# A grouped 1x1 convolution on one core: every full slot is stored in two halves

## The chip, the cores and the metric

The kernel runs on one core of one Trainium2 chip. The metric is the device time of one execution, in microseconds (us). Three executions of the kernel before took 477.21, 481.44 and 481.57 us, so its median is 481.44 us. One more execution was taken with the hardware profiler; it took 478.2 us, and all durations below are from that one.

## The reference

Inputs are an image `x` of 1 x 512 x 512 pixels with 192 channels in bf16, and weights `w` of 4 groups, 48 x 48 each. The kernel size is 1, so each pixel is by itself: its 192 channels are 4 groups of 48, and each group is multiplied by its own 48 x 48 matrix.

```python
B, H, W, C = x.shape                     # 1, 512, 512, 192
xg = xp.reshape(B, H, W, G, Cg)          # G = 4, Cg = 48, no padding
out = jnp.einsum('bhwgc,gcd->bhwgd', xg, w[0, 0])
return out.reshape(B, H, W, C)
```

There are 262,144 pixels of 384 bytes: 100.7 MB are read and 100.7 MB are written.

## The kernel before

**The ring.** All data passes through one buffer in SBUF, `ring`, of 128 partitions and 520 columns. A column is one pixel (384 bytes) in each partition. The ring is cut into 5 slots of 104 columns. The image is cut into pieces (`plan_pieces`), and the pieces fill the slots in turn: slot number n of the run lies in place n modulo 5. Slot 0 comes in four pieces of 8, 24, 32 and 40 columns (`HEAD`). Slots 6 and 13 are made of a piece of 40 columns and a "shared" piece, whose 64 columns lie in only some of the partitions. The last slot, number 20, has 36 columns. The 17 others are full: one piece of 104 columns each, 128 rows of 39,936 bytes, 4992 KB.

**What happens to a piece.** It is loaded into its place in the ring. TensorE (PE) takes it in groups of 4 columns: it transposes the group's channels into PSUM (L287), VectorE copies them to SBUF as `xT_sb` (L337), TensorE multiplies them by the weights into `o_ps` (L301), and ScalarE (ACT) copies the result back over the same four columns of the ring (L364). When enough columns have been written over, they are stored to the output. There are 529 groups. TensorE works on pairs of groups, and transposes one pair ahead of the pair that it multiplies.

**Who issues the transfers.** SP issues all loads but the shared ones, in order (L249). ACT issues all stores but the shared ones, in its own instruction stream, a group or two after the last copy that they need (L358). POOL issues the loads and stores of the two shared pieces (L221, with some tiny transfers at L219 ahead of them). The three have a DMA queue each: q1 for SP, q10 for ACT, q0 for POOL. Any transfer over 128 partitions is spread over the core's 16 DMA engines, 8 partitions each, and every engine serves all three queues.

**What waits for what.** A load may only write columns of the ring whose old contents have been stored: before it issues the load of piece p, SP waits (`wait_free`) for every store that covers the columns which p takes over from five slots before. `store_of` says which store covers which group. POOL does the same for a shared piece, two pieces ahead of the one in hand. POOL also collects the landings: it waits for a piece's load and then raises `ready` (L234), on which TensorE waits before its first transpose of the piece. POOL runs through the pieces in order, so a wait for a shared piece's place stands ahead of the report on the piece in hand.

**How stores are cut.** The list `stores` is made once, ahead of everything (lines 142 to 154). A piece is stored whole, with two exceptions: the last piece goes in parts of 16, 12 and 8 columns, and a full piece of the last three slots (`LATE = 3`) goes in two halves. Of the full slots that is true of numbers 18 and 19. The list decides what ACT issues and after which group, and how many semaphores SP and POOL wait for.

The functions that the change touches, with the line numbers of the profile:

Of the kernel before, what the change touches and what calls it, by code (L numbers as in the profile page):

```python
# [25 lines left out]
SLOT = 104  # L26
# [1 line left out]
COLS = SLOTS * SLOT  # L28
COL = 2 * C
HEAD = (8, 24, 32, 40)  # L30
LATE = 3
LAST_PARTS = (16, 12, 8)
LOOP = 2 * SLOT // 4
SHARED_AT = (6, 13)
# [48 lines left out]
def plan_pieces(npix):  # L83
    few = sum(rows * cols for _, rows, _, cols, _ in SHARED)
    at = list(SHARED_AT)
    if npix < len(at) * few + 128 * SLOT * (1 + at[-1]):
        at = []
    cols = (npix - few * len(at)) // 128
    assert cols % 4 == 0
    pieces, g, pix, n = [], 0, 0, 0  # L90
    while cols:
        if n in at:
            parts = [(SLOT - WIDE, None), (WIDE, SHARED)]
        elif n == 0 and cols >= SLOT:
            parts = [(s, None) for s in HEAD]
        else:
            parts = [(min(SLOT, cols), None)]
        for s, shares in parts:
            pieces.append(Piece(len(pieces), n, g, s, shares, pix))
            cols -= 0 if shares else s  # L100
            g, pix = pieces[-1].g1, pieces[-1].pix_end
        n += 1
    assert pix == npix
    return pieces


def bass_standalone__grouped__vision_kernel(nc, x, w, out):
# [5 lines left out]
    pieces = plan_pieces(npix)  # L113
# [27 lines left out]

    stores = []
    for p in pieces:
        late = pieces[-1].slot - p.slot
        half = p.size // 8 * 4
        parts = (p.size,)
        if p is pieces[-1] and p.size == sum(LAST_PARTS):
            parts = LAST_PARTS
        elif p.full and late < LATE and half:
            parts = (p.size - half, half)  # L150
        c = 0
        for n in parts:
            stores.append((p, c, c + n, p.g0 + (c + n) // 4))
            c += n
# [245 lines left out]
```

## Time and profile before

| | |
|---|---|
| median of three executions | 481.44 us (477.21 to 481.57) |
| profiled execution | 478.2 us |
| its span, first to last instruction | 476.2 us |
| TensorE clock granted, mean | 0.981 of full speed |
| busy: PE / ACT / VectorE | 435.7 / 398.7 / 254.1 us |
| moved by DMA | 201.50 MB, 423 GB/s over the span |
| full stores, 4992 KB | 15, median 46.7 us from issue to landing |
| half stores, 2496 KB | 4, median 22.5 us from issue to landing |
| full loads, 4992 KB | 17, median 33.8 us from issue to landing |

How to read the profile: it is of one execution on the core. PE is the matmul, PEld the weight load that goes beside it, DVE is VectorE, ACT ScalarE, POOL GpSimd; a name with q (SPq, ACTq) is the engine's instruction queue, where waits and DMA issues stand. "Busy tenths" cut the span into 40 equal slices, and each digit is the busy share of a slice in tenths, 9 being 90% or more. A line of waits reads: engine, what it was about to write, its line, an arrow to what ended the wait, and then the total us, the number of waits and the longest. A line of DMA issues reads: out<-in, the queue, how many, KB of each, and the median us from the issue to the landing of the last byte. KB are 1024 bytes, MB and GB are powers of ten.

### The profile page before, as it was taken

To read this page: it belongs to the slowest core of one execution; us is meant where nothing else is said; L and a number is where in the kernel's file an instruction comes from. 1 tells how busy PE (TensorE), PEld (TensorE's weight loads), DVE (VectorE), ACT (ScalarE), POOL (GpSimd) and SP (SyncE) were. 2 spreads that over 40 slices of the span, in tenths; PEclk is the share of its full clock that TensorE was granted. 3 is DMA by queue.
4 is the path that set the end of the run, shared out by engine and by line. 5 is a ranking of instruction groups with operands and counts; after the bars stand their busy time and mean duration, and the time that the engine had idled before them with its cause. 6 is when DMAs were issued, how large, how long until landed. Compare 5 with 4: busy or idle time off the path is not lost.

```text
span 476.2 us, 14571 instructions
## 1 busy us (share of the span) xinstructions
PE 435.7 (92%) x6358; PEld 394.8 (83%) x6358; DVE 254.1 (53%) x266; ACT 398.7 (84%) x530; POOL 10.0 (2%) x23
## 2 busy tenths in 40 slices
PE   5998899999999999999999999999998998988970
PEld 5887798888989888898888889889888897878860
DVE  2645455655555565555555555555554654554630
ACT  2988799989998998999899899989996998786980
POOL 1000000010000010000001000010000000000000
PEclk9999999999999999999999999999998999998995
DMA  8999999999999999999999999999999999999996
GB/s 345 430 432 426 427 436 438 429 418 424 423 413 429 430 443 426 425 438 433 433 429 430 434 437 424 436 429 437 423 404 437 429 423 426 423 438 439 413 431 284
DMA packets 8571, 201.50 MB, mean 423 GB/s; under 512 B 1664, under 2 KB 1664, under 8 KB 2304
## 3 DMA queue, kind: packets, MB, share of 16 engines
q1 hardware_dynamic: 3456, 97.72, 48.1%
q10 hardware_dynamic: 4240, 97.73, 47.9%
q0 software_dynamic: 864, 5.91, 3.0%
q8 instruction: 6, 0.10, 0.1%
q14 instruction: 5, 0.04, 0.0%
HBM read 100.69 MB, written 100.66 MB: 423 GB/s over the span
## 4 chain that ended last, share of the span: by engine, by line
PE 65%; DMA 22%; another core or an unknown queue 7%; issue 2%; ACT 1%; SPq 0%; POOL 0%; POOLq 0%
PE o_ps L301 38%; PE xT_ps L287 27%; DMA ring<-in_x_dram 13%; DMA out_dram<-ring 8%; ACT ring L364 1%; SPq L249 0%; POOL cur L219 0%; POOL out_dram L221 0%; POOLq L234 0%; SPq L55 0%
## 5 line engine op out<-in xcount | busy, mean ns | idle before, releaser
L364 ACT CAST ring<-o_ps 128x768 bf16<-128x768 f32 x529 | 397.4, 802 | 62.9 <-PE o_ps L301 55.4
L337 DVE COPY xT_sb<-xT_ps 128x1536 bf16<-128x1536 bf16 x265 | 253.4, 956 | 201.3 <-PE xT_ps L287 201.3
L301 PE MATMUL o_ps<-wt,xT_sb 128*128 128x144 bf16 (+1 forms) x3174 | 294.8, 235 | 7.5 <-issue 2.6
L301 PEld LDWEIGHTS o_ps<-wt,xT_sb 128*128 128x128 bf16 x3174 | 213.7, 98 | 45.4 <-ACT ring L364 30.2
L287 PE MATMUL xT_ps<-ident,ring 128*128 128x128 bf16 x3174 | 223.6, 221 | 14.5 <-POOLq L234 10.1
L287 PEld LDWEIGHTS xT_ps<-ident,ring 128*128 (+1 forms) x3174 | 192.2, 99 | 17.4 <-issue 17.2
L219 POOL DMA_DIRECT2D cur<-in_x_dram x7 | 4.2, 597 | 309.0 <-DMA out_dram<-ring 182.4
L261 PE MATMUL o_ps<-w_sb,esel 48*128 48x48 bf16 x10 | 0.6, 210 | 4.3 <-DMA w_sb<-in_w_dram 4.3
L261 PEld LDWEIGHTS o_ps<-w_sb,esel 48*128 48x128 bf16 x10 | 0.5, 110 | 4.2 <-issue 4.2
L331 DVE CAST wt<-o_ps 128x480 bf16<-128x480 f32 x1 | 0.7, 658 | 4.9 <-PE o_ps L261 4.9
L364 ACT ACT_TABLE_LOAD x1 | 1.3, 1283 | 1.3 <-PEq L385 1.3
L221 POOL DMA_DIRECT2D ring<-in_x_dram x4 | 2.3, 582 | 0.0
L221 POOL DMA_DIRECT2D out_dram<-ring x4 | 2.3, 576 | 0.0
L205 POOL TENSOR_SCALAR_AFFINE_SELECT esel<-esel 48x272 bf16<-48x272 bf16 x1 | 0.4, 402 | 0.0
L202 POOL MEMSET esel<- 48x272 bf16 x1 | 0.3, 317 | 0.3 <-POOLq L385 0.3
L209 POOL TENSOR_SCALAR_AFFINE_SELECT ident<-ident 128x128 bf16<-128x128 bf16 x1 | 0.3, 282 | 0.0
L203 POOL MEMSET ident<- 128x128 bf16 x1 | 0.2, 198 | 0.0
L385 POOL MEMSET const-float32-0.0<- 128x1 f32 x1 | 0.1, 98 | 0.3 <-issue 0.3
L385 POOL MEMSET const-bfloat16-1.0<- 128x1 bf16 x1 | 0.1, 101 | 0.0
L385 POOL MEMSET const-uint8-127<- 128x1 uint8 x1 | 0.1, 101 | 0.0
L385 POOL MEMSET const-float32-1.0<- 128x1 f32 x1 | 0.1, 98 | 0.0
## 6 DMA issues: line engine op xcount, KB each, us to landing
ring<-in_x_dram SPq DMA_DIRECT2D x17, 4992.0 KB, 33.8
out_dram<-ring ACTq DMA_DIRECT2D x15, 4992.0 KB, 46.7
out_dram<-ring ACTq DMA_DIRECT2D x4, 2496.0 KB, 22.5
ring<-in_x_dram SPq DMA_DIRECT2D x3, 1920.0 KB, 30.0
out_dram<-ring ACTq DMA_DIRECT2D x3, 1920.0 KB, 55.8
ring<-in_x_dram POOLq DMA_DIRECT2D x2, 1056.0 KB, 23.0
out_dram<-ring POOLq DMA_DIRECT2D x2, 1056.0 KB, 30.4
ring<-in_x_dram SPq DMA_DIRECT2D x1, 1728.0 KB, 29.8
```

Source lines behind the costliest of these rows:

```text
L202: gp.memset(esel[:], 1.0).then_inc(p0_sem, 1)
L205: gp.affine_select(out=esel[:], in_=esel[:], pattern=[[-1, ECOLS]], compare_op=AluOpType.is_equal, fill=0.0, base=ESHIFT, channel_multipli ...
L209: gp.affine_select(out=ident[:], in_=ident[:], pattern=[[-1, 128]], compare_op=AluOpType.is_equal, fill=0.0, base=0, channel_multiplier=1) ...
L219: gp.dma_start(cur[0:n, turns[0]], few).then_inc(cur_sem, 16)
L221: gp.dma_start(*((sbuf, dram) if inward else (dram, sbuf))).then_inc(done, 16)
L261: last = pe.matmul(o_ps[:, NOB - 1, col:col + CG], lhsT=esel[:, s0:s0 + 128], rhs=w_sb[:, g, :], start=True, stop=True, skip_group_check=True)
L287: last = pe.transpose(xT_ps[:, g % NXP, i * 128:(i + 1) * 128], xs, ident[:])
L301: last = pe.matmul(o_ps[:, v % NOB, c0_:c1_], lhsT=xs[:, i * 128:(i + 1) * 128], rhs=wt[:, WOFF[tc]:WOFF[tc] + (c1_ - c0_)], start=(tc == ...
L331: dve.tensor_copy(wt[:], o_ps[:, NOB - 1, 0:WCOLS]).then_inc(wc_sem, 1)
L337: dve.tensor_copy(xT_sb[pair % NXS][:, 0:n * 2 * UC].rearrange("p (g c) -> p g c", g=n), xT_ps[:, b0:b0 + n, 0:2 * UC]).then_inc(e_left, 1)
L364: act.copy(dst, o_ps[:, v % NOB:v % NOB + 2, 0:UC]).then_inc(o_left, 1)
L385: nc = _bacc.Bacc("TRN2", target_bir_lowering=False, num_devices=1)
```

## The change

The two halves are no longer kept for the last slots. Every piece that fills a slot of 104 columns is stored as two parts of 52 columns; the constant `LATE` goes. The last piece keeps its parts of 16, 12 and 8, and the pieces of the first slot, the 40 columns of slots 6 and 13 and the shared pieces are stored as before.

```diff
-LATE = 3
 LAST_PARTS = (16, 12, 8)
...
     stores = []
     for p in pieces:
-        late = pieces[-1].slot - p.slot
         half = p.size // 8 * 4
         parts = (p.size,)
         if p is pieces[-1] and p.size == sum(LAST_PARTS):
             parts = LAST_PARTS
-        elif p.full and late < LATE and half:
+        elif p.full and p.size == SLOT:
             parts = (p.size - half, half)
         c = 0
         for n in parts:
             stores.append((p, c, c + n, p.g0 + (c + n) // 4))
             c += n
```

ACT's stream has 15 more DMA issues: each of 15 full slots (numbers 1 to 5, 7 to 12 and 14 to 17) has one after its 13th group and one after its 26th, where it had one after the 26th. A half is 128 rows of 19,968 bytes. The streams of the other engines hold the same instructions. The lines behind the change move up by two. A load of a full slot now waits for two stores of the slot five before it; the 40 columns of slots 6 and 13 and the 36 of slot 20 wait for the first half of it alone.

## The prediction

> **What bounds the kernel now.** I read the slices first, then the DMA queues, then the waits, then stretches of my choosing. The slices and the queues, from the page:
>
> ```profile
> PE   5998899999999999999999999999998998988970
> DMA  8999999999999999999999999999999999999996
> ...
> q1 hardware_dynamic: 3456, 97.72, 48.1%
> q10 hardware_dynamic: 4240, 97.73, 47.9%
> q0 software_dynamic: 864, 5.91, 3.0%
> ```
>
> q1 carries SP's loads, q10 ACT's stores, q0 POOL's shared pieces. The shares add to 99.1% of the span (with 0.1% for instructions): the 16 DMA engines work 471.9 of 476.2 us. Of the 4.3 us left, some 2.6 lie before the first load moves. PE is busy too (92%), and the chain that ended last is 65% PE, which tempts one to call PE the bound. But PE ends at 462.0 us and the last store lands some 13 us later, and PE waits for loads near the end. The waits from 340 us on:
>
> ```profile
> PE xT_ps L287 <- POOLq L234: 8.2, 3, 3.1
> ```
>
> L234 is POOL's report that a piece has landed, and the chain shows the last of these to be the load issued at 391.90 that landed at 429.5. So PE waits for DMA, not DMA for PE. Stretches (columns: stretch, its length, busy time by engine, granted TensorE clock, DMA share, GB/s):
>
> ```profile
> 3.00:12.30 9.30, 6.88 (x74) 6.54 (x75) 3.41 (x4) 2.02 (x3) 0.00 (x0) 1.00 1.04 428
> 165.00:208.00 43.00, 41.97 (x624) 38.10 (x622) 24.68 (x27) 38.83 (x52) 2.28 (x4) 1.00 1.01 434
> 300.00:350.00 50.00, 48.85 (x728) 44.33 (x726) 28.86 (x31) 45.23 (x61) 2.27 (x4) 1.00 0.99 422
> 400.00:445.50 45.50, 39.36 (x560) 35.64 (x557) 22.34 (x24) 35.05 (x47) 0.00 (x0) 0.96 1.00 428
> 445.50:465.00 19.50, 15.80 (x224) 13.70 (x222) 8.87 (x10) 15.81 (x22) 0.00 (x0) 1.00 1.01 430
> ```
>
> The first row is loads alone (the first store is issued at 12.29), the last is stores alone (the last load lands at 445.5), the others are mixed: 428, 430 and 422 to 434 GB/s. So the engines move about 429 GB/s whatever the mix, and the time is bytes over that rate plus two short ends. The change moves the same bytes.
>
> **How two queues share an engine.** While the long loads of slots 1 to 4 run, the four small stores of slot 0 go beside them. Single issues, sizes and times to landing:
>
> ```profile
> out_dram<-ring ACTq DMA_DIRECT2D x1, 384.0 KB, 16.9
> out_dram<-ring ACTq DMA_DIRECT2D x1, 1152.0 KB, 26.9
> out_dram<-ring ACTq DMA_DIRECT2D x1, 1536.0 KB, 35.8
> out_dram<-ring ACTq DMA_DIRECT2D x1, 1920.0 KB, 42.9
> ```
>
> Issued at 12.29, 17.33, 23.86 and 33.12, they land at 29.2, 44.2, 59.7 and 76.0. The four loads (issued at 2.6 to 4.3, 26.4, 40.9, 55.8 and 71.7 us to landing) land at about 29, 44, 59 and 76: each store ends with one load, though it has a tenth to two fifths of its bytes. At half the bandwidth 0.39 MB would have taken 1.8 us, not 16.9. So each engine takes turns, a row of a store, a row of a load. A DMA has 144 packets (3456 over 24 loads), 9 an engine: 8 rows and one for the semaphore.
>
> **The change part by part.**
>
> *Turns.* The 15 full slots that were stored whole get rows of 19,968 B instead of 39,936. An engine moves 429/16 = 26.8 GB/s: 1.49 us a full row, 0.74 a half. Before, a load got every second row of equal size; its 8 rows need 8 x 2.98 = 23.8 us, and with the load ahead of it in the queue the median load lands after 33.8 us. After, a turn of both is 2.23 us: 8 turns are 17.9, with start and semaphore some 20 to 22 us. In that time only one half slot is stored; the other half, 8 x 0.74 = 5.9 us, then goes alone. 17.9 + 5.9 = 23.8, the old period. No byte is saved: loads land earlier, and since the bytes are the same, stores land later, by about half a slot's store, 6 us.
>
> *Who waits for the later stores.* SP's load of a slot waits for both halves of the slot five before, so it is issued about 6 us later and lands (33.8 - 21) - 6, some 7 us, earlier than now. The first pieces of slots 6 and 13 and the last load need the first half alone, which helps a little. POOL, before it reports slot 12 as landed, must wait for the whole store of slot 8 (it lands at 255.4 now, 261 then); PE needs slot 12 at about 274, so 12 us of cover stay. Slot 5's report waits likewise for slot 1 (96.4 now; its second half then some 10 us later), and is needed at about 122. Were that cover gone, PE would wait, with some two slots of stores (46.7 us to landing) still queued for the DMA engines.
>
> *PE.* With loads 7 us earlier the three late waits (8.2 us) go, and the slow matmuls after them (granted clock 0.66 from 430 to 435). PE ends some 7 us earlier. What is late next is the DMA queue: those 7 us become a longer drain, so I take nothing for it. At most what is idle behind the first load, 4.3 - 2.6 = 1.7 us, could be had.
>
> *ACT.* 15 more issues of 338 ns are 5.1 us on ACT, which idles 62.9. In the steady part ACT needs 2 x 0.773 us for a pair that takes PE 1.635 (two pairs every 3.27 us in the chain), so one issue is made up in four pairs; a half slot has 6.5. PE and DVE have the same instructions. Were that cover gone, PE would lose 5.1 us, less than the 13 us by which the last landing follows it.
>
> *15 more DMAs on q10*, 135 packets more on each engine. The nearest row is the half stores that run already, one behind the other at the end:
>
> ```profile
> out_dram<-ring ACTq DMA_DIRECT2D x1, 2496.0 KB, 25.0
> out_dram<-ring ACTq DMA_DIRECT2D x1, 2496.0 KB, 20.0
> ```
>
> Issued at 434.73 and 445.61, they land at 459.7 and 465.6 (the next at 471.5): 5.9 us apart for 2.556 MB, 433 GB/s. So a half store queued behind another costs nothing that shows. Upper bound in a queue: the second load, 24 columns, lands 3.14 us after the first; 1.18 MB at 429 are 2.75, so 0.39 a DMA, or 5.9 us for 15. Far bound: the first load, with nothing ahead of it, took 3.1 us for 0.92 us of bytes: 2.2 of its own, 33 us for 15. Below nothing: 433 against 429 is 0.9% on a quarter of the time, -1.0 us. I take +0.03 each, +0.5 us, by the nearest row, and keep -1 and +5.9 for the range.
>
> The Trainium skill (DMA: Bandwidth & Descriptors, "Anatomy of one DMA") gives every DMA a fixed cost of about 2.0 us; the lone first load agrees with its 2.2. Paid 15 times in line, that would be 30 us and a time of some 510. The page lays most of it to waiting for the last byte's receipt, and the queued half stores at 5.9 us agree that the next DMA hides it.
>
> **Sum.** Against the profiled execution of 478.2 us (span 476.2): bytes 0, PE 0, ACT 0, DMAs +0.5: 478.7. The runs shown are 477.21, 481.44 and 481.57, their mean 480.1, 1.9 above the profile. I lay the sum on that: 480.6, rounded to 480.5, 0.2% under the median. The three runs lie 0.9% apart, so 1% (4.8 us: under 476.6 or over 486.3) is about what can be told from no change.
>
> **Rivals.**
>
> *A, faster: the rate rises.* The late stretch with its PE waits runs at 422 (300 to 350) and 428 (350 to 445), the middle at 433 to 434. If loads in time lift these to 433, that is 50 x 11/433 + 95 x 5/433 = 2.4 us; with the 1.7 idle and the forecast's 0.5 not paid, 480.1 - 4.1 = 476.0. For it: a run with steadier loads might also fall nearer to the fastest of the three. Against: DMA share is 1.00 in the dips too. Chance 0.17.
>
> *B, slower: an added store costs its own time.* In the stretches where stores now run alone (5.9 us of every 23.8) no load fills a gap between one half and the next. It decides from (486.3 - 480.1)/15 = 0.41 us an added store, just above the 0.39 of the queued load and far below the 2.2 of the lone one. At 0.5 us: 487.6. For it: those stretches are new in the middle of the run. Against: the half stores 5.9 us apart, in just such a stretch. All of the skill's 30 us I give 0.01 of this case's 0.18.
>
> *C, the turns don't follow the rows*: engines share by bytes when both queues are long, loads still take some 33 us, and PE's three waits stay. DMA is as full as before: 480.5 again. Chance 0.10; the four pairs of landings speak against it.
>
> The forecast itself has 0.55. Faster: A, 0.17. Slower: B, 0.18. Within 1%: forecast and C, 0.65. The likeliest case alone spans 477 to 485 (the spread of the runs, and -1 to +3). For 8 in 10 I go out to A and B as priced: 474.5 to 488.
>
> **What the changed profile would show.** 34 stores of 2496 KB where there are 4, and none of 4992 KB. Median load to landing 20 to 24 us instead of 33.8. Late PE waits for L234 near zero, PE's last matmul at 453 to 457. DMA share still 9 in every slice, 423 GB/s over the span within 1%. q10 with 15 x 144 = 2160 packets more, 6400, and its share within half a point of 47.9%. Wrong would be a slice of DMA below 9 in the middle, q10's share up by over 1 point (B), or a mean over 428 GB/s (A).

## The result, and the profile after

| | before | after |
|---|---|---|
| median of twelve executions | 476.59 us (475.40 to 481.57) | 482.47 us (480.73 to 483.55) |
| ratio to before | | 1.0101, 95% interval 1.0070 to 1.0133 |
| profiled execution | 478.2 us, span 476.2 | 482.83 us, span 480.9 |

The change makes the kernel 1.0% slower. The number forecast, 480.5 us, lies near the measured one and the range holds it, but the forecast was for no change that can be told, and it rested on three executions of before that turned out to be high ones. Between the two profiled executions the forecast was +0.5 us and the measured difference is +4.6 us; the medians of twelve lie 5.9 us apart. (The ratios here leave out executions of a kernel that fell over 1.5% behind its fastest; the profiles of experiments 5 and 15 are of such executions, and only their packets are read.)

The page of after, the span in 40 slices and the DMA queues (packets, MB, share of 16 engines):

```profile
span 480.9 us, 14605 instructions
...
PE   4989799999999999999999999999999599999920
...
DMA  8999999999999999999999999999999999999994
...
DMA packets 10731, 201.50 MB, mean 419 GB/s; under 512 B 1904, under 2 KB 1904, under 8 KB 2544
...
q1 hardware_dynamic: 3456, 97.72, 47.9%
q10 hardware_dynamic: 6400, 97.74, 47.8%
q0 software_dynamic: 864, 5.91, 2.9%
```

As before, DMA stands at 9 in every slice to the last; q10 has the 2160 more packets that were forecast, and its share has not grown. And yet the mean rate is 419 GB/s instead of 423. By this page the engines are as busy as they were and move less. The one slice that differs is the last: 4 instead of 6.

The same page's DMA issues (how many, KB each, median us from issue to landing):

```profile
ring<-in_x_dram SPq DMA_DIRECT2D x17, 4992.0 KB, 23.8
out_dram<-ring ACTq DMA_DIRECT2D x34, 2496.0 KB, 50.3
```

The loads land after 23.8 us instead of 33.8, which is the turn by rows as the prediction has it. But a half store now takes 50.3 us, longer than a whole one took (46.7). PE's waits from 340 us on, and from the timeline the longest of them with the issue of the load it waited for:

```profile
PE xT_ps L285 <- POOLq L232: 5.1, 2, 4.8
```

```profile
360.67 7.75 SPq L247 DMA_DIRECT2D ring<-in_x_dram  x2
...
384.69 1.36 PE L285 MATMUL xT_ps<-ident,ring 128*128 128x128 bf16 x12 [4.75 <-POOLq L232]
```

One long wait, of 4.8 us, is left: PE stands still until the load of slot 17, issued at 360.67, has landed at 384.3. Before, that load was issued at 351.79.

The stretches of after that answer to those shown of before, and then its last 9 us (columns: stretch, length, busy time by engine, granted TensorE clock, DMA share, GB/s):

```profile
165.00:208.00 43.00, 41.93 (x624) 38.00 (x622) 24.67 (x27) 38.90 (x52) 2.29 (x4) 1.00 1.00 427
300.00:350.00 50.00, 48.85 (x728) 44.34 (x726) 28.73 (x30) 45.25 (x62) 2.28 (x4) 1.00 1.01 429
400.00:445.50 45.50, 44.39 (x659) 40.16 (x657) 26.51 (x28) 41.16 (x56) 0.00 (x0) 1.00 1.00 426
445.50:465.00 19.50, 13.84 (x197) 11.99 (x195) 7.56 (x9) 14.06 (x19) 0.00 (x0) 0.96 1.02 435
472.00:474.00 2.00, 0.00 (x0) 0.00 (x0) 0.00 (x0) 0.00 (x0) 0.00 (x0) 0.50 0.78 320
474.00:476.00 2.00, 0.00 (x0) 0.00 (x0) 0.00 (x0) 0.00 (x0) 0.00 (x0) 0.50 0.34 139
476.00:478.00 2.00, 0.00 (x0) 0.00 (x0) 0.00 (x0) 0.00 (x0) 0.00 (x0) 0.50 0.16 67
478.00:480.90 2.90, 0.00 (x0) 0.00 (x0) 0.00 (x0) 0.00 (x0) 0.00 (x0) 0.50 0.04 18
```

and the last 6 us of before:

```profile
470.00:472.00 2.00, 0.00 (x0) 0.00 (x0) 0.00 (x0) 0.00 (x0) 0.00 (x0) 0.50 0.76 313
472.00:474.00 2.00, 0.00 (x0) 0.00 (x0) 0.00 (x0) 0.00 (x0) 0.00 (x0) 0.50 0.38 155
474.00:476.00 2.00, 0.00 (x0) 0.00 (x0) 0.00 (x0) 0.00 (x0) 0.00 (x0) 0.50 0.11 44
```

Between 165 and 208 us, where PE is as busy as before, the rate fell from 434 to 427 GB/s. The last rows are the first sign of where the time went. A share of 1/16 is 0.06: from 476 us on, one to three of the 16 engines work, and the others have ended. In after this tail runs from 474 to 480.4 us, in before from 472 to 475.7. So a mean over 16 engines was the wrong thing to look at.

### Engine by engine

The trace lists each packet with its queue, size, start and duration, but not its engine. The packets can be laid out on 16 engines, so that each engine does one after the other (with some 3 ns of overlap from one to the next, which makes a busy time up to 2 us longer than the time it fills) and takes its own 8 rows of every transfer, in order. In this layout, made from 4.6 us on, no engine is ever idle for more than 1.3 us before its last store. What is said of single engines below rests on it; the landings are read directly from the semaphores' updates, of which each transfer has one per engine.

An undisturbed row of 39,936 bytes takes 1476 ns, a half row of 19,968 takes 742, the semaphore's packet 9 (the commonest durations). With these every engine has a fixed amount of work. What its packets take beyond that is called its *stall* here.

```
profiled executions, us, from 4.6 us on           before                  after
mean of 16 engines: fixed work                     464.5                   465.7
                    stall                            4.4                     5.8
                    instruction fetches              0.5                     0.4
                    busy, the sum                  469.4                   471.9
busiest engine:     fixed work                     465.4                   466.5
                    stall                            5.5                    10.1
                    instruction fetches              1.4                     0.9
                    busy, the sum                  472.4                   477.5
time of the execution less the busiest engine        5.8                     5.3
last store lands, first / median / last engine     471.1 / 472.7 / 475.7   472.4 / 474.7 / 480.4
slot 12's store,  first / median / last engine     342.2 / 346.9 / 351.8   337.6 / 350.0 / 360.6
```

The fixed work grows by 1.1 us: 120 more half-row pairs by 8 ns and 15 more semaphore packets by 9 ns on each engine. The rest of the +4.6 us is stall, and it counts where it is largest: the busiest engine lost 5.5 us before and 10.1 after, while the median of the 15 ordinary ones went from 2.7 to 4.7. (A sixteenth engine, of which more at the end, stalls 19 us in both and is spared the shared pieces.) The profiled execution of before lies 1.6 us above its median, so a usual one has probably stalled less: the same stores with another first slot (experiment 12 below, 475.53 us) lose 2.9 us on the worst ordinary engine. The row of slot 12 shows the same lag in the middle of the run, and what it does to PE: SP may issue the load of slot 17 only when the *last* engine has stored slot 12, at 360.6 us, though half the engines had stored it by 350.0.

The stalls are not spread evenly. Rows of two engines are often slow together: after 70 us, 114 rows of after (the sixteenth engine's left out) are stalled by 200 ns or more, 44.9 us together. Of this, 61% is on rows that have a partner, a row of the same queue on another engine at the same time and slowed about as much; with the times of the other engines shifted by 5 to 55 us, 1 to 20% would have one. In before it is 77 rows, 32.2 us, 73% with a partner. At the worst both take twice their time: at 125.8 us two half rows take 742 + 779 ns each. So such pairs hold most of the long stalls of both kernels. But of the 12.7 us that after adds in such rows they are only 3.9 (61% of 44.9 less 73% of 32.2); for the rest no partner was found.

### The profile page after: what moved, and what is told of

The parts are those of the page before. It is cut to its first block, busy times and chain, and to the rows that moved or that the text cites. A ratio compares the mean times of both kernels' runs of the same rounds, so it can differ in the third digit from the quotient of the medians.

```text
span 480.9 us, 14605 instructions
## 1 busy us (share of the span) xinstructions
PE 434.6 (90%) x6358; PEld 393.8 (82%) x6358; DVE 254.0 (53%) x266; ACT 398.7 (83%) x530; POOL 10.0 (2%) x23
## 3 DMA queue, kind: packets, MB, share of 16 engines
q10 hardware_dynamic: 6400, 97.74, 47.8%
## 4 chain that ended last, share of the span: by engine, by line
PE 53%; another core or an unknown queue 23%; DMA 17%; issue 2%; ACT 1%; SPq 0%; POOLq 0%
PE o_ps L299 31%; PE xT_ps L285 22%; DMA out_dram<-ring 10%; DMA ring<-in_x_dram 6%; ACT ring L362 1%; SPq L247 0%; SPq L54 0%; POOLq L232 0%
## 5 line engine op out<-in xcount | busy, mean ns | idle before, releaser
L299 PEld LDWEIGHTS o_ps<-wt,xT_sb 128*128 128x128 bf16 x3174 | 212.7, 98 | 46.7 <-ACT ring L362 30.9
## 6 DMA issues: line engine op xcount, KB each, us to landing
ring<-in_x_dram SPq DMA_DIRECT2D x17, 4992.0 KB, 23.8
out_dram<-ring ACTq DMA_DIRECT2D x34, 2496.0 KB, 50.3
ring<-in_x_dram SPq DMA_DIRECT2D x3, 1920.0 KB, 23.8
```

The lines of the kernel that those rows point to most:

```text
L299: last = pe.matmul(o_ps[:, v % NOB, c0_:c1_], lhsT=xs[:, i * 128:(i + 1) * 128], rhs=wt[:, WOFF[tc]:WOFF[tc] + (c1_ - c0_)], start=(tc == ...
```

## The experiments

Each ran with the kernel before on the same chip; ratios are to that. The letters in the expectations are the theories as they stood when they were written, and each text says what it expects. The diffs show the lines that matter; "..." stands for lines left out.

### 1, 2: equal rows for loads, and a later issue for stores

Loads of full slots in halves too, both after the same waits:

```diff
+    def load_parts(p):
+        return ((0, SLOT // 2), (SLOT // 2, SLOT)) if p.full and p.size == SLOT else ((0, None),)
...
                 wait_free(wq, p)
-                for _, dram, sbuf in transfers(xf, p, SYNC):
-                    sp.dma_start(sbuf, dram).then_inc(ld_sem[p.i], 16)
+                for c0, c1 in load_parts(p):
+                    for _, dram, sbuf in transfers(xf, p, SYNC, c0, c1):
+                        sp.dma_start(sbuf, dram).then_inc(ld_sem[p.i], 16)
```

> The full loads are cut into two halves as well, so that a row of a load and a row of a store are equal again (19,968 B). Theory T (turns): the loss of the changed kernel comes from stores getting the smaller row in each turn; the store queue grows, the 16 engines drift apart in it (the last store's slowest engine lands 5.7 us after the median engine, 3.0 before). With equal rows loads take some 34 us again, the slowest engine ends about 3 us behind the median, and only the fixed cost of rows stays, 2 x 1.1 us: ratio to the kernel before 1.003 to 1.006. Theory R (rows): each added row and semaphore packet costs, in its fixed 8 to 9 ns and in longer stalls, 4 to 5 us for 2160 packets; with twice as many the ratio is 1.015 to 1.025.

Halves as in after, but both issued at the end of their slot:

```diff
         for n in parts:
-            stores.append((p, c, c + n, p.g0 + (c + n) // 4))
+            due = p.g1 if len(parts) == 2 and p.slot < 18 else p.g0 + (c + n) // 4
+            stores.append((p, c, c + n, p.g0 + (c + n) // 4, due))
...
-                while todo and todo[0][3] < g:
+                while todo and todo[0][4] < g:
```

> Halves as in the changed kernel, but for slots 1 to 17 both are issued together after the slot's last group, as the whole store was. Theory T and theory R: the rows are the same, so the ratio stays 1.007 to 1.013 and loads land in some 24 us. Rival E (early issue): what costs is that the first half is issued ten us sooner and sits beside the load; then the ratio falls to 1.000 to 1.004.

Experiment 1 measured 1.0100 (1.0053 to 1.0147), between the ranges of T and R; one of its five executions took 485.50 us, and the four others, at 478.64 to 479.90, are 0.5 to 0.8% above the median of before. Experiment 2 measured 1.0154 (1.0136 to 1.0171), above every range written down for it. From the page of experiment 1, the slices of DMA and the issues:

```profile
DMA  8999999999999999999999999999999999999977
...
ring<-in_x_dram SPq DMA_DIRECT2D x34, 2496.0 KB, 53.8
out_dram<-ring ACTq DMA_DIRECT2D x34, 2496.0 KB, 22.4
```

With equal rows the roles turn: the half loads wait in their queue (53.8 us) and the stores go through quickly. The stalls are gone, a median of 1.3 us an engine instead of 4.7, and the engines land the last store within 475.0 to 476.9 us. But PE now waits 16.9 us for loads:

```profile
PE xT_ps L289 <- POOLq L235: 16.9, 6, 5.6
```

so PE's last matmul ends at 469.4 us instead of 462.0, and the engines run out of stores before it (columns as above; the share of the DMA engines is 0.31):

```profile
460.00:465.00 5.00, 4.83 (x72) 4.18 (x70) 2.84 (x4) 4.41 (x7) 0.00 (x0) 1.00 0.31 132
```

So the gain is given back. Experiment 2 keeps the 23.8 us of the loads and the stalls (7.6 us on the worst engine). It isn't the early issue of the first half that costs: issued late, the halves cost more, 1.0154 against 1.0101.

### 3, 9, 13, 14: halves in a part of the run

```diff
-        elif p.full and p.size == SLOT:
+        elif p.full and p.size == SLOT and (p.slot < 10 or p.slot >= 18):       # 3: slots 1 to 9
+        elif p.full and p.size == SLOT and p.slot >= 10:                        # 9: slots 10 to 19
+        elif p.full and p.size == SLOT and (p.slot < 5 or p.slot >= 18):        # 13: slots 1 to 4
+        elif p.full and p.size == SLOT and (5 <= p.slot < 10 or p.slot >= 18):  # 14: slots 5 to 9
```

(Slots 18 and 19 are in halves before, too.)

> Halves for slots 1 to 5 and 7 to 9 only (and 18 and 19, as before); slots 10 to 17 are stored whole. Theory T: from slot 10 on turns are equal again, the engines' distance at the end is that of the kernel before (3 us from median to last), ratio 1.000 to 1.004. Theory R: half of the added rows, half of the loss, 1.004 to 1.007.

> The complement of the early halves: slots 1 to 9 are stored whole, slots 10 to 19 in halves. With early halves alone the loss was whole (1.0137) and the last engine's lag was there before slot 10. If lags come only from the loads that begin on an empty queue, each costs alike and the late half brings its share: worst engine's stalls 7 to 10 us, ratio 1.004 to 1.010. If the early part of the run is what matters (first fills, the shared piece at 97 us), the late half costs little: 1.000 to 1.004.

> Only slots 1 to 4 in halves, beside 18 and 19. T (a load that begins on an empty queue costs the engines about 0.3 us on the mean and the unluckiest about 1 us, so the loss goes with the number of such loads): the loads of slots 5 to 9 alone begin on an empty queue, 4 of the 7 to 8 that the kernel with slots 1 to 9 in halves has before 300 us; ratio 1.004 to 1.009, the loads that follow directly stalled under 0.1 us. U (once the engines have been put out of step early in the run, the rest follows by itself): ratio 1.010 to 1.015, as with slots 1 to 9, and stalls go on after the last load that began on an empty queue.

> Only slots 5 to 9 in halves, beside 18 and 19. T: loads of slots 10 to 14 begin on an empty queue, the other half of those; ratio 1.004 to 1.009, and the two parts together come near the 1.0137 of slots 1 to 9. U: what counts is that it begins early; ratio 0.998 to 1.004, as with the late halves (1.0019).

```
halves in slots        added stores   ratio (95% interval)        us lost per added store
1 to 9    (3)                     8   1.0137 (1.0119 to 1.0155)   0.82
10 to 19  (9)                     7   1.0019 (0.9996 to 1.0042)   0.13
1 to 4    (13)                    4   1.0113 (1.0090 to 1.0136)   1.35
5 to 9    (14)                    4   1.0067 (1.0041 to 1.0093)   0.80
all       (after)                15   1.0101 (1.0070 to 1.0133)   0.32
```

(Loss: the ratio's excess by the 476 us of before.) Experiment 3 went against everything expected of it: the early half of the change alone carries the whole loss. Issues in the page of experiment 9, then of experiment 3:

```profile
ring<-in_x_dram SPq DMA_DIRECT2D x17, 4992.0 KB, 29.6
```

```profile
ring<-in_x_dram SPq DMA_DIRECT2D x17, 4992.0 KB, 29.2
```

The loads land as early in both, and yet 3 loses 6.5 us and 9 loses 0.9 (for 9, the second of the two cases in its text). The packets agree: the worst ordinary engine stalls 9.2 us in experiment 3, nearly all of it before 300 us, and 3.8 in experiment 9. Four slots at the start cost as much as all fifteen. Against their expectations: 1 to 4 came out as U had it (set off early), not as T had it (in proportion to the loads begun on an empty queue); 5 to 9 came out as T had it, not as U; and the two together exceed the 1.0137 of both. So the loss neither goes with the number of half stores nor is set off only at the very start. It is the dearer, the earlier the halves come. The profiled execution of experiment 13 was the fastest of its six (478.41, median 481.40), so its packets, 5.9 us on the worst engine, show little of that loss.

### 4: the mirror, loads in halves and stores whole

The edit of experiment 1, on the kernel before.

> The other way round: full loads in halves, stores as in the kernel before. Theory T: stores get the larger row, full loads take 40 us and more, TensorE waits for loads on every slot from the middle of the run on, and the store queue runs short; slower than the changed kernel, ratio 1.01 to 1.03. Theory R: 17 x 144 added packets, about the same as the changed kernel's 2160, ratio 1.008 to 1.013, whatever the queue they are on.

It measured 1.0321 (1.0299 to 1.0343), a little above T's range and far above R's. Waits, and the slices of the page:

```profile
PE xT_ps L291 <- POOLq L237: 27.6, 5, 9.5
```

```profile
DMA  8999999999999999999999999999999999999557
...
ring<-in_x_dram SPq DMA_DIRECT2D x34, 2496.0 KB, 48.0
out_dram<-ring ACTq DMA_DIRECT2D x15, 4992.0 KB, 23.2
```

Now the stores have the long rows and two thirds of each engine, as the turns by row say: 23.2 us, and the loads 48.0. Loads are what PE needs, so PE waits 27.6 us, and the queue of stores runs dry. The stalls come too: a median of 8.3 us on an engine, 13.3 on the worst. Unequal rows come with stalls whichever way round they are.

### 6, 7: equal rows without PE's waits

Experiment 6 is 1, with each half load waiting for the half store alone that it replaces:

```diff
-                wait_free(wq, p)
...
                 for c0, c1 in load_parts(p):
+                    wait_free(wq, p, c0, c1)
...
```

> Loads and stores of full slots in halves, and each half load waits only for the half store whose place it takes, so that loads are issued half a slot sooner than where both halves of a load wait for both stores. Theory S: q1 never runs dry, load rows lose 0.01 to 0.05 us an engine; what kept the kernel with both in halves at 1.01 were 16.9 us of TensorE waits for late loads and idle DMA engines at the end (2 to 4 us each). These shrink to under 10 and under 2 us: time 474 to 478, ratio 0.997 to 1.004. Theory R (rows): 1.008 to 1.02, as with both in halves.

Experiment 7 makes every full slot of two pieces, so that loads, waits, reports to PE and stores all go by 52 columns (and the shared pieces are issued three pieces ahead, not two):

```diff
-AHEAD = 2
+AHEAD = 3
...
-            parts = [(min(SLOT, cols), None)]
+            parts = [(SLOT // 2, None)] * 2 if cols >= SLOT else [(cols, None)]
```

> Full slots are made of two pieces of 52 columns each: loads, stores, the waits for free places and TensorE's waits for landed data all go by halves (POOL looks three pieces ahead instead of two, to issue the shared loads where it did). Theory S as above, and TensorE starts on a half as soon as it has landed, 12 us sooner than on the whole: TensorE waits under 5 us in the second half of the run, DMA engines idle under 1 us before the end, time 473.5 to 477, ratio 0.994 to 1.001. Theory R (rows): 1.008 to 1.02.

Experiment 6 measured 1.0052 (1.0009 to 1.0094), with 14.6 us of PE's waits for loads left where S expected under 10 (one of its six executions took 483.06 us, the others 477.96 to 479.42). Experiment 7 measured 1.0000 (0.9966 to 1.0033), as S had it. GB/s in the 40 slices, experiment 7, then before, then after:

```profile
GB/s 347 416 412 434 427 428 433 435 432 427 430 432 432 427 430 429 430 433 432 428 432 427 431 431 426 430 430 432 426 426 431 436 432 433 432 428 427 430 430 286
```

```profile
GB/s 345 430 432 426 427 436 438 429 418 424 423 413 429 430 443 426 425 438 433 433 429 430 434 437 424 436 429 437 423 404 437 429 423 426 423 438 439 413 431 284
```

```profile
GB/s 340 457 411 430 422 432 415 414 419 431 424 424 422 421 433 423 434 440 420 428 447 401 433 425 427 427 430 425 424 425 441 443 417 427 420 421 432 438 422 194
```

From the fifth slice to the one before the last, experiment 7 stays within 426 to 436; before dips to 404 and after to 401, and from the seventh slice to the fourteenth, 72 to 168 us, after lies at 414 to 431. Such stretches are part of the loss, and "9" in the slices of DMA hides them. All stores and loads of experiment 7 are halves, so its rows cost 2.3 us more of fixed work than before's, and it makes them good: the median stall is 1.2 us. So half rows by themselves, and more of them and more DMAs than in after, do not cost what after loses. Unequal rows do, or what comes with them: in after the load queue, and in experiment 4 the store queue, also runs empty at times, and these runs do not part the one from the other.

### 10, 11, 12: is it chance of timing?

After and before with the first slot's pieces in another order (10 and 12), and after with parts of 56 and 48 columns (11):

```diff
-HEAD = (8, 24, 32, 40)
+HEAD = (8, 24, 40, 32)
```

```diff
-        half = p.size // 8 * 4
+        half = 48
```

> The changed kernel with the last two pieces of slot 0 swapped (8, 24, 40, 32 columns): the same bytes, rows and DMAs, a little other timing. Theory P: what costs is that rows of two engines meet and slow each other to as little as half speed, the engine that meets most often sets the end, and which engines meet hangs on where they stand to one another when loads begin anew. Then a shift without work changes the loss by 2 us and more in at least one of this run and the next two: ratio anywhere in 1.000 to 1.020, and the profiled time is the worst engine's busy time plus 5 to 6 us. Theory S (each load on an empty queue costs a set time): 1.007 to 1.013.

> The changed kernel with parts of 56 and 48 columns instead of 52 and 52: the same number of rows and DMAs. Theory P: 1.000 to 1.020, not the same loss but by chance; stalls of 200 ns and more still come mostly two engines at a time. Theory S: 1.007 to 1.013.

> The kernel before with the same swap in slot 0. Its loads follow one another without a gap for most of the run. Theory P: fewer meetings, but some around the shared pieces and late loads: 0.995 to 1.008, likely moved by 1 us or more. Theory S: 0.998 to 1.002.

They measured 1.0114 (1.0086 to 1.0142), 1.0103 (1.0076 to 1.0131) and 0.9968 (0.9935 to 1.0002). P wanted the loss to move by 2 us or more in one of them, and it did not (against after's 1.0101 the first two lie within 0.6 us, and the third is 1.5 us under before); S's range holds for 10 and 11. Which engines meet when is different in each, but the loss of the halves stays where it was, and the kernel with whole stores stays at before's time (0.3% under it, which isn't resolved; no kernel here is shown to be faster than before). The worst ordinary engine stalls 10.1, 10.5 and 2.9 us. So it isn't an unlucky timing of this one program.

All kernels whose packets were laid out, by their profiled executions:

```
                        time     busiest engine   time - busiest   stall of the 15: median, max
before                  478.20   472.4            5.8              2.7    6.9
after                   482.83   477.5            5.3              4.7   10.1
1  both in halves       479.30   472.3            7.0              1.3    4.7
2  late issue           482.07   476.3            5.8              5.3    7.6
3  slots 1 to 9         482.47   476.7            5.8              4.7    9.2
4  loads in halves      494.03   480.9           13.1              8.3   13.3
6  half waits           479.07   473.0            6.1              1.0    2.0
7  pieces of 52         477.36   472.9            4.5              1.2    3.0
9  slots 10 to 19       477.61   470.9            6.7              2.7    3.8
10 after, other head    483.25   477.5            5.8              5.2   10.1
11 parts of 56 and 48   482.34   477.3            5.0              4.9   10.5
12 before, other head   475.53   470.2            5.3              2.0    2.9
13 slots 1 to 4         478.41   472.8            5.6              3.2    5.9
```

The time is the busiest engine's work and 4.5 to 7 us more, in all but experiment 4, whose engines run out of work for longer than those of 1.

### 5, 15: loads that begin on an empty queue

In after the loads land 10 us sooner than before, mostly before SP can issue the next, so the load queue is empty when most loads begin. Of the sixteen loads from slot 5 on that is true of eleven: they are stalled by 0.06 to 0.73 us an engine (mean 0.28), largely in their first four rows; the five others, which follow another directly, by 0.01. (Slot 2's load, earlier, follows another directly beside short rows of stores and is stalled by 0.42.) To try the empty queue by itself, the kernel before was made to hold some loads until the one ahead had landed: those of slots 8, 10 and 12 in experiment 5, of slot 9 in experiment 15.

```diff
+DRY = (8, 10, 12)                                                # 15: (9,)
...
                 wait_free(wq, p)
+                if p.slot in DRY:
+                    prev = pieces[p.i - 1]
+                    wq.wait(ld_sem[prev.i], 16 * len(prev.on(SYNC)))
```

> The kernel before, whole stores, but SP issues the loads of slots 8, 10 and 12 only when the load before has landed, so that q1 is empty on all engines as each of them begins. Theory S (a load that begins on an empty queue stalls): in the kernel before, loads that follow one another directly lose 0.01 to 0.06 us an engine on their rows, in the changed kernel those that begin on an empty queue lose 0.16 to 0.73. So loads 8, 10 and 12 lose 0.2 to 0.5 us an engine and 0.5 to 1.3 on the worst engine, loads 9 and 11 stay at 0.01 to 0.06, with no row or DMA added; the time rises by 0.5 to 3 us, ratio 1.001 to 1.006. Rival R2 (the stalls come with half rows of stores): all five stay at 0.01 to 0.06, ratio 0.999 to 1.001.

> The kernel before, all stores whole but 18 and 19; SP waits for the load of slot 8 to land before it issues that of slot 9, so that one load begins on an empty queue with whole rows in the other. T: its rows are stalled by 0.1 to 0.7 us an engine, the worst engine by 0.5 to 1.5, and the loads after it that follow directly by under 0.1; ratio 1.000 to 1.004. V (it takes short rows of the stores beside the load, not the empty queue): its rows are stalled by under 0.05 us an engine, as those of loads that follow directly; ratio 0.998 to 1.002.

Experiment 5 took 479.43 us once and 492.58 to 497.39 in five others, and gives no ratio. Experiment 15 measured 1.0013 (0.9994 to 1.0032), with two of thirteen executions at 496.25 and 497.58 left out. In the profiled executions, which took 492.58 and 496.25, the held loads were stalled by 0.07, 0.52, 0.05 and 0.01 us an engine. One of four is what S and T expected; the other three are near R2's and V's. Before has such rows too: the loads of slots 7, 16, 18 and 19, which follow others directly, are stalled by 0.54, 0.48, 0.24 and 0.33, where the first of the two texts has 0.01 to 0.06 for such loads. So an empty queue is not shown to be what makes engines meet; short rows beside it may be needed, and this stays open. In the packets of experiment 15's profiled execution three engines lose some 2 us in every 20, from 200 us on, just after the held load, for most of the rest of the run. Whether holding loads brings on executions of 492 us and more, which no run of before shows, is open too.

### 8: more DMAs, rows whole

To double the stores without short rows, each whole store of before was issued as two of 64 partitions:

```diff
+                    if two(i):
+                        for r0 in (0, 64):
+                            act.dma_start(dram[r0:r0 + 64], span(p.at + c0, p.at + c1, r0, r0 + 64)).then_inc(st_sem[i], 16)
...
```

> The kernel before, but each of the 15 whole stores is issued as two DMAs of 64 partitions, both after the slot's last group: 15 DMAs and semaphore counts more, as in the changed kernel, but rows of 39,936 B as in a load (and other partitions on each engine, which may matter by itself). Theory T (unequal rows let q1 run dry): loads keep to some 34 us, rows keep their stalls, ratio 0.999 to 1.004. Theory R (the number of DMAs): as the changed kernel, 1.007 to 1.013.

It measured 1.1755 (1.1692 to 1.1818), which none of the theories had. The page's slices and mean:

```profile
DMA  8999999999999999999999999999999999999831
...
DMA packets 8812, 201.50 MB, mean 361 GB/s; under 512 B 1905, under 2 KB 1905, under 8 KB 2545
```

The full rows of stores take 1876 ns on the mean instead of 1487, and one in ten takes 2985 or more, twice 1476. The Trainium skill (DMA: Bandwidth & Descriptors, "The descriptor swizzle") says that in a transfer over 128 partitions each engine writes to a port of the SBUF of its own. Over 64 partitions each engine has four rows instead of eight, so the partitions fall to other engines. In that page's list partitions 0 to 63 lie on eight of the 16 ports, so two engines would share one; the doubled rows agree with it, though the page speaks of writes where these are stores, and no run here shows a port. As a test of the number of DMAs it fails, for it changed something larger. It shows most plainly what the share of busy time can hide: engines that are busy all the time (9 in nearly every slice) at 361 GB/s. That its cause is the one of after is not shown.

## Why the prediction was wrong

**Right.** DMA bounds the kernel. The engines take turns by rows: packet after packet, an engine's queue reads 39,936, 3,072, 39,936, 3,072 bytes while small stores run beside long loads, loads landed after 23.8 us (forecast 20 to 24), and experiment 4 shows the mirror of it. The Trainium skill (DMA: Bandwidth & Descriptors, "Queues, rings and completion order") has the turns, but lets an engine drain typically 9 to 17 descriptors of a queue before it switches; here it is one row each, and the measurement decides. ACT's 15 issues stayed hidden (PE waits 0.5 us for ACT in both kernels), q10 has 6400 packets at 47.8%, no slice of DMA is below 9 in the middle.

**The step that failed** is the one on which the sum stands: "the time is bytes over that rate plus two short ends". The rate was read from means over 16 engines. The end is set by the busiest of them, and after raises its work by 5.1 us where the mean engine's rises by 2.5. Within the sum, the term "15 more DMAs, +0.03 each, +0.5 us, by the nearest row" was mis-sized as well: the fixed work of rows and semaphores measured +1.1 us, 0.07 a DMA. That is twice the forecast and a quarter of the loss. The half stores 5.9 us apart, from which it was taken, ran alone at the end, where no load's rows stand beside theirs. A row that shows one queue alone can't price what two queues do together. (The section of the Trainium skill from which the 2.0 us are taken is on DMAs that GpSimd issues; ACT's, behind one another, cost 0.07 us each in fixed work.)

**Stores later by 6 us, loads earlier by 7, PE ending at 453 to 457.** The stores came 9 to 10 us later: slot 8's at 265.8 (255.4 before; forecast 261), slot 12's at 360.6 (351.8). The engines' medians moved by less, 346.9 to 350.0 for slot 12; it is again the slowest engine. So the load of slot 17 was issued 9 us later, one of PE's waits remained (8.2 us went to 5.1, not to near zero), and PE's last matmul ends at 460.1 instead of 462.0.

**The base.** The sum was laid on the mean 480.1 of three executions, two of which lay 5 us above the median of twelve. So the base was 3.5 us too high, and the change, +0.5 us instead of the 5.9 between the medians, 5.4 too low; the two cancel in part, and 480.5 came within 2 us of the measured 482.47. That is luck and no merit of the working.

**The rivals.** B had the sign, and not the mechanism: it priced each added store at 0.41 us or more, but an added store costs 1.35 us in slots 1 to 4 and 0.13 in slots 10 to 19, and experiment 7, with still more half transfers, costs nothing. A (the rate rises with loads in time) had a part: the late stretch rose from 422 to 429 GB/s between 300 and 350 us, but others fell, from 434 to 427 between 165 and 208. C is out: the loads landed after 23.8 us, not 33.

**What is shown, and what is open.** Shown: the end follows the busiest engine, and most of what that engine adds is stall (4.6 us, beside 1.1 of fixed work); most long stalls, before and after, fall on two engines at the same time; with equal rows in both queues they are all but gone (experiments 1, 6, 7), with unequal ones they are there either way round (after, 4), whatever the timing of the rest (10, 11); halves in the first four slots are enough for the loss (13). Open: what the engines share when they meet, and whether it is the meeting that slows them; what the added stalls without a partner come from; whether the emptied load queue sets it off, for which only the difference within after speaks (0.28 against 0.01 us a load) while three of four held loads do not; and why the same halves cost so much less after slot 9.

## What to carry to other kernels

Where two queues share the DMA engines, give loads and stores rows of equal size, or change both together: an engine alternates row for row, so a halved row cuts its queue's share from a half to a third while both are full, and here it also cost 1% through stalled engines. In a kernel that DMA bounds, compare the first and the last engine's landing of a store before trusting a mean rate or a "9" in the DMA slices; the last engine ends the run and holds up the next load. Don't split a 128-partition transfer by partitions to get more DMAs (1.18 here).

## What the runs showed of the hardware that was not expected

- Rows of two engines were slowed to half speed at the same time (742 + 779 ns each), while both count as busy. What slows them is not shown.
- A row costs about 8 ns by itself (2 x 742 against 1476 ns) and a semaphore's packet 9 ns, so cutting rows in half at these sizes costs 0.5%; queued half stores are 5.9 us apart.
- One engine of the 16 is slower in every kernel laid out: its store rows take some 110 to 120 ns longer each (50 to 60 for half rows), 15 to 21 us in the run. It is the engine that has no rows of the shared pieces, which spares it 14.4 us, so it ends with the others.
- Instruction fetches take an engine's time: six of 16 KB, some 0.9 us each, fall on single engines, and one of them lay on the busiest engine of after.
